# Two x tiles loaded by rows instead of columns, and their first blocks handled ahead of the rest

## The chip, the cores and the metric

The kernel runs on one NeuronCore of one Trainium2 chip. The time is the device time of one execution in microseconds; less is better. Engines are named as the profile names them: PE is TensorE, DVE is VectorE, ACT is ScalarE, POOL is GpSimd, SP is SyncE, whose queue here only issues DMAs.

## The reference: what is computed

A layernorm without scale and shift, and a two-layer MLP with a tanh GELU behind it. x is 2048 rows of 1024, the hidden width is 3584, everything is bf16 at the borders.

```python
B, S, D, F = 1, 2048, 1024, 3584
y = _layernorm(x, axis=-1)
h = _gelu(jnp.einsum("bsd,df->bsf", y, w1) + b1)
return jnp.einsum("bsf,fd->bsd", h, w2) + b2
```

## The kernel before, in words

The 2048 rows are cut into 16 tiles of 128 rows; four tiles make a block, and there are four blocks. For each block, a first stage makes the hidden values transposed: for each of 28 groups of 128 hidden columns, 8 matmuls (one per 128 of D) add up into one PSUM bank, and ACT applies bias and GELU into `hT_sb`. A second stage multiplies `hT_sb` by w2, DVE adds b2, and SP stores. All weights stay in SBUF after one load. The matmuls of the first stage need the normalised x transposed (`yT_sb`), with D on the partitions.

For blocks 1 to 3 DVE normalises and transposes in the shadow of the matmuls. Block 0 has no such shadow, so its four tiles are handled in a special way. For tiles 0 and 1, x is only centred before the matmuls; the division by the standard deviation is done later, by a multiplication of the finished PSUM rows with `rbc_sb` (the reciprocal deviations, L346). What the front of the kernel does is this.

- Loads. All four engines' programs are lists of operations with named signals. The loop at L203 loads tiles 0 and 1 in two halves each: columns 0 to 511 through SP's queue (`x0_0`, `x1_0`), columns 512 to 1023 through ACT's (`x0_1`, `x1_1`), all 128 rows, 1024 bytes a row. Behind them on SP's queue come the pieces of w1, with x2 and x3 between them (`LOADS`).
- Row sums. ACT sums columns 0 to 511 of tile 0 and then of tile 1 (L400, a copy with an accumulator, signals `sa0`, `sa1`). DVE sums columns 512 to 1023: of tile 0 by a scaled copy with an accumulator (L403, `sd0`), of tile 1 by an addition of one 256-column half to the other with an accumulator (L417, `sd1`). An accumulator is read out by an instruction of its own.
- Centring. `centre` (L410) subtracts both partial sums, already divided by 1024, from x into `c_sb`. Tile 0 is done in two pieces, blocks 0 to 1 and 2 to 7 (a block is 128 columns), and tile 1 in two, blocks 0 to 3 and 4 to 7. DVE's written order is: sum of tile 0, centring of tile 0 (both pieces), sum of tile 1, centring of tile 1 (both pieces), `bn_stats` of tile 0 (L229), tile 2 (L426 sum, L430 centring), tile 3.
- Transposes. PE transposes the 128x128 blocks of `c_sb` into PSUM (`pe_T`, L303), in the groups of `GROUPS_0`, `GROUPS_1` and `GROUPS_2` (first block, last block plus one, PSUM bank), and ACT copies each group into `yT_sb` (L309). Tile 3 is transposed by DVE and copied by DVE and ACT (L453, L462, L467).
- PE's order. 37 small matmuls on constants whose result nobody reads (`fill`, L289), the first group of tile 0, two more of these, the two other groups of tile 0, and then what `OPEN` lists: an entry `(1, None)` is all transposes of tile 1, `(2, None)` those of tile 2, and `(t0, t1, d0, d1)` is the first stage's matmuls for hidden groups 0 to 3, tiles t0 to t1-1, D-blocks d0 to d1-1 (L329). So (0, 1, 0, 2) is 8 matmuls of 128 columns, (1, 2, 0, 2) 8 more, (0, 2, 2, 6) 16 of 256, (0, 2, 6, 8) 8 of 256. Then hidden groups 4 to 7 for three tiles (384 columns), the rest of groups 0 to 7, and groups 8 to 27 with 512 columns.
- After the transposes of tile 1 ACT's list has the square of tile 1, after those of tile 2 the squares of tiles 2 and 3 (`square`, L437), with small operations of POOL behind each.

The order of DVE's later work (normalising the next blocks, the multiplications of L346, the output additions of L389) is made by a small planner from estimates of when PE and the DMAs are done; PE's clock in it starts at `T_PE_START`.

Of the kernel before, what the change touches and what calls it, by code (L numbers as in the profile page):

```python
# [5 lines left out]
ACT = mybir.ActivationFunctionType  # L6
ALU = mybir.AluOpType
# [4 lines left out]
P = 128  # L12
# [5 lines left out]
R1 = 8  # L18
N_FILL_A = 37
N_FILL_C = 2  # L20
OPEN = ((1, None), (0, 1, 0, 2), (1, 2, 0, 2), (0, 2, 2, 6), (2, None), (0, 2, 6, 8))
CEN_0 = (0, 2, 8)
CEN_1 = (0, 4, 8)
GROUPS_0 = ((0, 2, 7), (2, 5, 4), (5, 8, 5))
GROUPS_1 = ((0, 4, 6), (4, 8, 7))
GROUPS_2 = ((0, 2, 4), (2, 5, 5), (5, 8, 6))
COPY_ACT = ((0, 1), (0, 2), (0, 3), (1, 2), (1, 3), (2, 3))
LOADS = (0, 1, 2, -2, 3, -3, 4, 5, 6, 7)
NOB = 2
# [59 lines left out]
def bass_standalone__mixer_channel_mlp__prompt_kernel(  # L89
# [8 lines left out]
    xf = x.rearrange("b s d -> (b s) d")  # L98
    of = out.rearrange("b s d -> (b s) d")
    ST, D = xf.shape  # L100
# [7 lines left out]
    HC = D // 2  # L108
    NRAW = TPB
# [29 lines left out]
    with ExitStack() as es:  # L139
# [4 lines left out]
        x_sb = sb("x_sb", [P, NT, D], BF16)  # L144
        yT_sb = sb("yT_sb", [P, 2, DT, TB], BF16)
        hT_sb = sb("hT_sb", [P, FT, TB], BF16)
        o_sb = sb("o_sb", [P, NOB, D], BF16)
        b2_sb = sb("b2_sb", [P, D], BF16)
        c_sb = sb("c_sb", [P, NRAW, D], BF16)
# [10 lines left out]
        sum_sb = sb("sum_sb", [P, NRAW + 2], F32)  # L160
# [10 lines left out]
        act = _Prog("s_act")  # L171
# [6 lines left out]
        x_ev = {}  # L178

        def dma(dst, src, sig, nbytes, q=None):  # L180
            (q or sp).op(lambda e, dst=dst, src=src: e.dma_start(dst, src), sig=sig, sem="d_" + sig, inc=16)
            dma_bytes[0] += nbytes
            est[sig] = DMA_T0 + dma_bytes[0] / DMA_BYTES_PER_US
# [18 lines left out]

        for i in range(2):  # L203
            for h, q in enumerate((sp, act)):
                dma(x_sb[:, i, h * HC:(h + 1) * HC], xf[i * P:(i + 1) * P, h * HC:(h + 1) * HC],
                    f"x{i}_{h}", P * HC * 2, q)
        for o in LOADS:
            load_x_tile(-o) if o < 0 else load_w1(o)
        sp.op(None, waits=["b1z"])
# [7 lines left out]
        for b in range(2, NB):  # L217
# [4 lines left out]
                sig="ident")  # L222
# [4 lines left out]

        def op_stats(i, h):
            return (lambda e, i=i, h=h: e.bn_stats(st_sb[:, i, 6 * h:6 * (h + 1)], x_sb[:, i, h * HC:(h + 1) * HC]),  # L229
                    [x_ev.get(i, f"x{i}_{h}")], f"st{i}_{h}", 0.65)  # L230

        def op_aggr(i, to=None):
            to = rstd_sb if to is None else to
# [6 lines left out]
        y_ev = {}  # L240
# [8 lines left out]
        def ln_seq(tiles):  # L249
            seq = []  # L250
            prev = None
            for i in tiles:
                for h in range(2):
                    seq.append(op_stats(i, h))
                    if h == 0 and prev is not None:
                        seq.append(op_norm(prev))
                seq.append(op_aggr(i))
                prev = i
            seq.append(op_norm(prev))
            return seq  # L260
# [20 lines left out]
        def dve_put(o):  # L281
            dve.op(o[0], waits=o[1], sig=o[2])
# [4 lines left out]
        def fill(n, gate=None):  # L287
            for _ in range(n):
                pe.op(lambda e: e.matmul(ps[:, 0, 0:P], lhsT=one, rhs=one, start=True, stop=True),  # L289
                      waits=[gate] if gate else [])  # L290

        def pe_T(i, group, src):
            blk, t = divmod(i, TPB)
            j0, j1, bank = group
            bap = psb[:, bank, :]
            evs = yT_ev.setdefault(i, [None] * DT)
            for j in range(j0, j1):
                waits = []
                if j == j0:
                    waits = ["ident"] + ([bank_read[bank]] if bank in bank_read else [])  # L300
                if j == j0 or y_ev[i][j] != y_ev[i][j - 1]:
                    waits.append(y_ev[i][j])
                pe.op(lambda e, j=j, o=(j - j0) * P: e.transpose(  # L303
                    out=bap[:, o:o + P], in_=src[:, j * P:(j + 1) * P], identity=ident[:, :]),
                    waits=waits, sig=(f"tp{i}_{j0}" if j == j1 - 1 else None))
                evs[j] = f"te{i}_{j0}"
            psrc = bap[:, 0:(j1 - j0) * P].rearrange("p (j s) -> p j s", j=j1 - j0)
            dst = yT_sb[:, blk % 2, j0:j1, t * P:(t + 1) * P]
            act.op(lambda e, dst=dst, psrc=psrc: e.copy(out=dst, in_=psrc), waits=[f"tp{i}_{j0}"], sig=f"te{i}_{j0}")  # L309
            bank_read[bank] = f"te{i}_{j0}"  # L310
            pe_t[0] += (j1 - j0) * 0.056
# [4 lines left out]
        def new_unit():  # L316
            u = unit_n[0]
            unit_n[0] += 1
            bank = u if u < NBANK else (u - NBANK) % NRING
            w = bank_gelu.get(bank, bank_read.get(bank))  # L320
            return bank, ([w] if w else [])
# [74 lines left out]
            store_last[(ob, region)] = sev  # L396

        act.op(lambda e: e.preload_act_table(ACT.Gelu_apprx_tanh))
        for i in range(2):
            act.op(lambda e, i=i: e.activation(out=hT_sb[:, 2 * NRAW + i, :], in_=x_sb[:, i, 0:HC], func=ACT.Copy,  # L400
                                               scale=1.0 / D, accum_out=sum_sb[:, 2 * i:2 * i + 1]),
                   waits=[f"x{i}_0"], sig=f"sa{i}")
        dve_put((lambda e: e.tensor_scalar(out=o_sb[:, 0, HC:D], in0=x_sb[:, 0, HC:D], scalar1=1.0 / D, scalar2=0.0,  # L403
                                           op0=ALU.mult, op1=ALU.add, accum_out=sum_sb[:, 1:2]),
                 ["x0_1"], "sd0"))

        def centre(i, cuts):
            y_ev[i] = []
            for j0, j1 in zip(cuts[:-1], cuts[1:]):
                dve_put((lambda e, a=j0 * P, b=j1 * P: e.tensor_scalar(  # L410
                    out=c_sb[:, i, a:b], in0=x_sb[:, i, a:b], scalar1=sum_sb[:, 2 * i:2 * i + 1],
                    scalar2=sum_sb[:, 2 * i + 1:2 * i + 2],
                    op0=ALU.subtract, op1=ALU.subtract), [f"sa{i}", f"sd{i}", f"x{i}_0"], f"y{i}_{j0}"))
                y_ev[i] += [f"y{i}_{j0}"] * (j1 - j0)

        centre(0, CEN_0)
        dve_put((lambda e: e.tensor_tensor_reduce(out=o_sb[:, 1, 0:HC // 2], in0=x_sb[:, 1, HC:HC + HC // 2],  # L417
                                                  in1=x_sb[:, 1, HC + HC // 2:D], op0=ALU.add, op1=ALU.add,
                                                  scale=1.0 / D, scalar=0.0, accum_out=sum_sb[:, 3:4]),
                 ["x1_1"], "sd1"))  # L420
        centre(1, CEN_1)
        pool.op(lambda e: e.tensor_tensor(out=tot_sb[:, :], in0=sum_sb[:, 2:3], in1=sum_sb[:, 3:4], op=ALU.add),
                waits=["sa1", "sd1"], sig="tot1")

# [40 lines left out]
        def t3_act():  # L465
            for k, (src, dst) in enumerate(c3_act):
                act.op(lambda e, src=src, dst=dst: e.copy(out=dst, in_=src), waits=["t3"],  # L467
                       sig="ta3" if k == len(c3_act) - 1 else None)

        for q in range(4):  # L470
            dve_put((lambda e, q=q: e.transpose(out=b1h_sb[32 * q:32 * (q + 1), :],
                                                in_=b1r_sb[0:32, 32 * q:32 * (q + 1)]), ["b1"], f"b1t{q}"))
        dve_put((lambda e: e.tensor_copy(out=b1_sb[:, :], in_=b1h_sb[:, :]), ["b1t3"], "b1c"))
        for q in range(4):
            rsrc = rs_sb[32 * q:32 * (q + 1), :].unsqueeze(2).broadcast_to([32, NRAW, 32])
            dve_put((lambda e, q=q, rsrc=rsrc: e.transpose(
                out=rbc_sb[32 * q:32 * (q + 1), :, 32 * q:32 * (q + 1)], in_=rsrc),
                ["rstd0"] + [f"rs{i}" for i in range(1, NRAW)], f"rq{q}"))
        for q in range(4):
            f = q ^ 1  # L480
            dve_put((lambda e, q=q, f=f: e.tensor_copy(
                out=rbc_sb[32 * q:32 * (q + 1), :, 32 * f:32 * (f + 1)],
                in_=rbc_sb[32 * f:32 * (f + 1), :, 32 * f:32 * (f + 1)]), [f"rq{f}"], f"rx{q}"))
        for h in range(2):
            f = h ^ 1
            dve_put((lambda e, h=h, f=f: e.tensor_copy(
                out=rbc_sb[64 * h:64 * (h + 1), :, 64 * f:64 * (f + 1)],
                in_=rbc_sb[64 * f:64 * (f + 1), :, 64 * f:64 * (f + 1)]),
                [f"rx{2 * f}", f"rx{2 * f + 1}"], "rbc" if h == 1 else None))

        fill(N_FILL_A)
        pe_T(0, GROUPS_0[0], c_sb[:, 0, :])
        fill(N_FILL_C)
        pe_T(0, GROUPS_0[1], c_sb[:, 0, :])
        pe_T(0, GROUPS_0[2], c_sb[:, 0, :])
        pe_t[0] = T_PE_START
        wave = [new_unit() for _ in range(R0)]
        for st in OPEN:
            t = st[0]
            if st[1] is None:  # L500
                for g in (GROUPS_2 if t == 2 else GROUPS_1):
                    pe_T(t, g, c_sb[:, t, :])
                if t == 1:
                    square(1)
                else:
                    square(2)
                    square(3)
                    t3_act()
                continue
            t0, t1, d0, d1 = st  # L510
            for dt in range(d0, d1):
                for r in range(R0):
                    pe_cell(0, r, t0, t1, wave[r][0], wave[r][1] if t0 == 0 and dt == 0 else [], None, dts=[dt])
# [43 lines left out]
        while ci < len(crit) or fi < len(fills):  # L557
            take_crit = fi >= len(fills)
            if not take_crit and ci < len(crit):
                rel_f, _, blk_f = fills[fi]  # L560
                if crit[ci][0] <= max(t_dve, rel_f) + CRIT_SLACK and blk_f > crit[ci][2]:
                    take_crit = True
            if take_crit:
                rdy, o, _ = crit[ci]
                ci += 1
            else:
                rdy, o, _ = fills[fi]
# [46 lines left out]
```

## Time and profile before

| | us |
|---|---|
| median of 3 runs | 397.56 (397.53 to 397.56) |
| the profiled execution | 397.73 |
| its span, first to last instruction | 396.5 |
| PE busy | 393.6 (99%) |
| DVE, ACT, POOL busy | 160.5, 88.1, 11.0 |
| first matmul that uses data of x and w1 | 6.88 after the span's start |
| four later first and second stages each | 48.35 |

Starts are counted from the span's start. A row of the timeline gives start, length, engine, line, operation, what it writes and reads, and how many neighbours it covers; in brackets is how long the engine had been idle, and on what it waited. The chain of waits lists the work that ended last, in order of time, with start and length. The length of a matmul includes its way through the array; matmuls that follow each other overlap, so the distance from start to start is what one costs. The profile's page gives the mean granted clock of PE as 1.00.

### The profile page before, as it was taken

The numbers are of one execution on the slowest core, as the hardware profiler recorded it, in microseconds if no ns is written. First come the engines' busy times: TensorE is split into PE (matmuls) and PEld (weight loads), VectorE is DVE, ScalarE is ACT, GpSimd is POOL, SyncE is SP. The second block draws the span as 40 slices with busy tenths as digits, with TensorE's granted clock in tenths as the row PEclk, the third lists the DMA queues.
The fourth block names the chain that finished last, engine by engine and source line by source line (L and its number), as shares of the span: only waits on it lengthen the run. The fifth ranks groups of instructions, "written<-read, shape, count | busy, mean of one in ns | idle before, by whom it ended". The sixth has DMA issues, their size and how long they took to land.

```text
span 396.5 us, 4568 instructions
## 1 busy us (share of the span) xinstructions
PE 393.6 (99%) x1955; PEld 187.7 (47%) x1955; DVE 160.5 (40%) x344; ACT 88.1 (22%) x137; POOL 11.0 (3%) x29
## 2 busy tenths in 40 slices
PE   8999999999999999999999999999999999999998
PEld 8754444444444444444444444444444444444445
DVE  5968898988999505987100000001100000001011
ACT  6663430000143442000024433100003334400000
POOL 1301100001000100000000000000000000000000
DMA  7999930000000000000000000000000000000000
GB/s 265 370 386 387 387 143 13 28 26 14 28 0 0 2 0 0 29 13 28 26 13 2 0 0 2 13 13 28 15 25 15 0 2 0 0 15 26 13 28 26
DMA packets 16349, 23.62 MB, mean 60 GB/s; under 512 B 1098, under 2 KB 8778, under 8 KB 16330
## 3 DMA queue, kind: packets, MB, share of 16 engines
q1 hardware_dynamic: 16042, 23.08, 16.4%
q8 instruction: 15, 0.25, 0.3%
q10 hardware_dynamic: 288, 0.26, 0.2%
q14 instruction: 4, 0.03, 0.0%
HBM read 19.14 MB, written 4.19 MB: 59 GB/s over the span
## 4 chain that ended last, share of the span: by engine, by line
PE 98%; DVE 0%; issue 0%
PE ps L329 49%; PE ps L378 49%; PE ps L303 0%; DVE c_sb L410 0%; DVE o_sb L417 0%; DVE o_sb L389 0%; DVE sum_sb L417 0%
## 5 line engine op out<-in xcount | busy, mean ns | idle before, releaser
L329 PE MATMUL ps<-yT_sb,w_sb 128*128 128x512 bf16 (+3 forms) x968 | 194.5, 363 | 0.0
L378 PE MATMUL ps<-w_sb,hT_sb 128*128 128x512 bf16 (+2 forms) x924 | 194.1, 373 | 0.0
L329 PEld LDWEIGHTS ps<-yT_sb,w_sb 128*128 128x128 bf16 x968 | 92.6, 98 | 100.7
L378 PEld LDWEIGHTS ps<-w_sb,hT_sb 128*128 128x128 bf16 x924 | 89.3, 98 | 104.5
L349 ACT ACTIVATE hT_sb<-ps,b_sb 128x512 bf16<-128x512 f32 x112 | 76.3, 687 | 254.8 <-PE ps L329 231.6
L389 DVE TENSOR_TENSOR o_sb<-ps,b_sb 128x512 bf16<-128x512 f32 (+2 forms) x33 | 22.3, 675 | 198.8 <-PE ps L378 198.7
L276 DVE STREAM_TRANSPOSE yT_sb<-x_sb 32x256 bf16<-32x256 bf16 x192 | 83.7, 436 | 20.7 <-PE ps L329 17.7
L346 DVE TENSOR_TENSOR ps<-ps,rbc_sb 128x512 f32<-128x512 f32 x28 | 18.9, 697 | 6.4 <-PE ps L329 5.6
L229 DVE BATCH_NORM_STATS2 st_sb<-x_sb 128x6 f32<-128x512 bf16 x26 | 17.2, 670 | 0.1
L234 POOL TENSOR_TENSOR rstd_sb<-mv_sb,nhalf 128x1 f32<-128x1 f32 x12 | 6.6, 548 | 113.8 <-DVE mv_sb L237 113.8
L244 DVE TENSOR_SCALAR x_sb<-x_sb,mv_sb,rstd_sb 128x1024 bf16<-128x1024 bf16 x12 | 6.5, 543 | 2.5 <-POOL rstd_sb L234 2.0
L289 PE MATMUL ps<-const-bfloat16-1.0 128*128 128x128 bf16 x39 | 4.5, 310 | 0.8 <-PEq L599 0.8
L289 PEld LDWEIGHTS ps<-const-bfloat16-1.0 128*128 128x128 bf16 x39 | 4.1, 145 | 0.8 <-issue 0.8
L309 ACT COPY yT_sb<-ps 128x384 bf16<-128x384 bf16 (+2 forms) x8 | 3.3, 489 | 1.7 <-PE ps L303 1.7
L237 DVE BATCH_NORM_AGGREGATE mv_sb<-st_sb 128x2 f32<-128x15 f32 x13 | 2.8, 219 | 0.8
L303 PE MATMUL ps<-ident,c_sb 128*128 128x128 bf16 x24 | 2.5, 240 | 0.2 <-DVE c_sb L410 0.2
L467 ACT COPY yT_sb<-o_sb 32x256 bf16<-32x256 bf16 x6 | 2.4, 402 | 0.1
L437 ACT ACTIVATE hT_sb<-x_sb,sum_sb 128x1024 bf16<-128x1024 bf16 x2 | 2.3, 1162 | 0.0
L462 DVE COPY yT_sb<-o_sb 32x256 bf16<-32x256 bf16 x10 | 2.2, 219 | 0.2
L403 DVE TENSOR_SCALAR_CACHE_REDUCE o_sb<-x_sb 128x512 bf16<-128x512 bf16 x1 | 0.7, 687 | 3.8 <-DMA x_sb<-in_x_dram 3.8
L303 PEld LDWEIGHTS ps<-ident,c_sb 128*128 128x128 bf16 x24 | 1.8, 108 | 0.8 <-issue 0.4
L444 POOL TENSOR_TENSOR rs_sb<-ve_sb,nhalf 128x1 f32<-128x1 f32 x3 | 1.7, 559 | 0.2
(31 smaller groups left out, 17.4 us busy)
## 6 DMA issues: line engine op xcount, KB each, us to landing
w_sb<-in_w_dram SPq DMA_DIRECT2D x4, 1792.0 KB, 18.4
w_sb<-in_w_dram SPq DMA_DIRECT2D x2, 2048.0 KB, 15.8
out_dram<-o_sb SPq DMA_DIRECT2D x31, 128.0 KB, 1.7
x_sb<-in_x_dram SPq DMA_DIRECT2D x3, 1024.0 KB, 14.8
w_sb<-in_w_dram SPq DMA_DIRECT2D x8, 256.0 KB, 5.2
w_sb<-in_w_dram SPq DMA_DIRECT2D x1, 1024.0 KB, 9.0
x_sb<-in_x_dram SPq DMA_DIRECT2D x2, 256.0 KB, 5.0
x_sb<-in_x_dram ACTq DMA_DIRECT2D x2, 128.0 KB, 3.1
```

The source lines that it names most:

```text
L229: return (lambda e, i=i, h=h: e.bn_stats(st_sb[:, i, 6 * h:6 * (h + 1)], x_sb[:, i, h * HC:(h + 1) * HC]), [x_ev.get(i, f"x{i}_{h}")], f"s ...
L234: pool.op(lambda e, i=i, to=to: e.tensor_tensor(out=to[:, i:i + 1], in0=mv_sb[:, i, 1:2], in1=nhalf[:, i:i + 1], op=ALU.pow), waits=[f"mv{ ...
L244: return (lambda e, i=i: e.tensor_scalar(out=x_sb[:, i, :], in0=x_sb[:, i, :], scalar1=mv_sb[:, i, 0:1], scalar2=rstd_sb[:, i:i + 1], op0= ...
L276: res.append((lambda e, src=src, dst=dst: e.transpose(out=dst, in_=src), waits, (f"tr{i}" if lastop else None), 0.47))
L289: pe.op(lambda e: e.matmul(ps[:, 0, 0:P], lhsT=one, rhs=one, start=True, stop=True), waits=[gate] if gate else [])
L303: pe.op(lambda e, j=j, o=(j - j0) * P: e.transpose(out=bap[:, o:o + P], in_=src[:, j * P:(j + 1) * P], identity=ident[:, :]), waits=waits, ...
L309: act.op(lambda e, dst=dst, psrc=psrc: e.copy(out=dst, in_=psrc), waits=[f"tp{i}_{j0}"], sig=f"te{i}_{j0}")
L329: pe.op(lambda e, b=b, r=r, dt=dt, n0=n0, n1=n1, bank=bank: e.matmul(ps[:, bank, n0:n1], lhsT=w1_sb[:, dt, r * P:(r + 1) * P], rhs=yT_sb[: ...
L346: crit.append((est[sig], (lambda e, bank=bank: e.tensor_tensor(out=ps[:, bank, 0:n], in0=ps[:, bank, 0:n], in1=rb, op=ALU.mult), [sig, "rb ...
L349: act.op(lambda e, r=r, bank=bank: e.activation(out=hT_sb[:, r, :], in_=ps[:, bank, :], func=ACT.Gelu_apprx_tanh, bias=b1_sb[:, r:r + 1], ...
L378: pe.op(lambda e, st=st, ft=ft, c0=c0, c1=c1, bank=bank: e.matmul(ps[:, bank, 0:c1 - c0], lhsT=hT_sb[:, ft, st * P:(st + 1) * P], rhs=w2_s ...
L389: crit.append((est[sig], (lambda e, ob=ob, c0=c0, c1=c1, bank=bank: e.tensor_tensor(out=o_sb[:, ob, c0:c1], in0=ps[:, bank, 0:c1 - c0], in ...
```

## The change

The four loads of tiles 0 and 1 become row halves: rows 0 to 63 through SP's queue and 64 to 127 through ACT's, each row whole (2048 bytes). Everything that reads tile 0 or 1 now waits for both halves. Tile 0 is summed as tile 1 is: ACT takes columns 0 to 383 (`SA0`) and DVE adds the two halves of the other 640 to each other with an accumulator; tile 1 stays at 512 and 512. DVE's order becomes: sum of tile 0, centring of its blocks 0 to 1, sum of tile 1, centring of its blocks 0 to 3, then tile 0's blocks 2 to 7, then tile 1's blocks 4 to 7. PE's order is spelled out by groups in `OPEN`: after the two extra small matmuls come tile 1's first group, tile 0's second, the 8 matmuls of (0, 1, 0, 2), tile 0's third group, tile 1's second, the 8 of (1, 2, 0, 2), the 16 of (0, 2, 2, 6), tile 2, and (0, 2, 6, 8). ACT's copies follow the order of the transposes.

```diff
-OPEN = ((1, None), (0, 1, 0, 2), (1, 2, 0, 2), (0, 2, 2, 6), (2, None), (0, 2, 6, 8))
+OPEN = (("T", 1, 0), ("T", 0, 1), (0, 1, 0, 2), ("T", 0, 2), ("T", 1, 1), (1, 2, 0, 2), (0, 2, 2, 6), ("T", 2, 0), ("T", 2, 1),
+        ("T", 2, 2), (0, 2, 6, 8))
+SA0 = 384
...
-                dma(x_sb[:, i, h * HC:(h + 1) * HC], xf[i * P:(i + 1) * P, h * HC:(h + 1) * HC],
-                    f"x{i}_{h}", P * HC * 2, q)
+                h0 = h * (P // 2)
+                dma(x_sb[h0:h0 + P // 2, i, :], xf[i * P + h0:i * P + h0 + P // 2, :], f"x{i}_{h}", P * D, q)
...
-                    [x_ev.get(i, f"x{i}_{h}")], f"st{i}_{h}", 0.65)
+                    [x_ev[i]] if i in x_ev else [f"x{i}_0", f"x{i}_1"], f"st{i}_{h}", 0.65)
...
+        def sums(i, na):
+            n2 = (D - na) // 2
+            act.op(lambda e: e.activation(out=hT_sb[:, 2 * NRAW + i, 0:na], in_=x_sb[:, i, 0:na], func=ACT.Copy,
+                                          scale=1.0 / D, accum_out=sum_sb[:, 2 * i:2 * i + 1]),
+                   waits=[f"x{i}_0", f"x{i}_1"], sig=f"sa{i}")
+            return (lambda e: e.tensor_tensor_reduce(out=o_sb[:, i, 0:n2], in0=x_sb[:, i, na:na + n2],
+                                                     in1=x_sb[:, i, na + n2:D], op0=ALU.add, op1=ALU.add,
+                                                     scale=1.0 / D, scalar=0.0, accum_out=sum_sb[:, 2 * i + 1:2 * i + 2]),
+                    [f"x{i}_0", f"x{i}_1"], f"sd{i}")
...
+        sd = [sums(0, SA0), sums(1, HC)]
+        dve_put(sd[0])
+        centre(0, *CEN_0[0:2])
+        dve_put(sd[1])
+        centre(1, *CEN_1[0:2])
+        centre(0, *CEN_0[1:3])
+        centre(1, *CEN_1[1:3])
...
         fill(N_FILL_A)
-        pe_T(0, GROUPS_0[0], c_sb[:, 0, :])
+        pe_T(0, GROUPS[0][0], c_sb[:, 0, :])
         fill(N_FILL_C)
-        pe_T(0, GROUPS_0[1], c_sb[:, 0, :])
-        pe_T(0, GROUPS_0[2], c_sb[:, 0, :])
```

More of the change, by code (lines that the diff above doesn't have):

```diff
@@ L20 @@
 N_FILL_C = 2
-OPEN = ((1, None), (0, 1, 0, 2), (1, 2, 0, 2), (0, 2, 2, 6), (2, None), (0, 2, 6, 8))
+OPEN = (("T", 1, 0), ("T", 0, 1), (0, 1, 0, 2), ("T", 0, 2), ("T", 1, 1), (1, 2, 0, 2), (0, 2, 2, 6), ("T", 2, 0), ("T", 2, 1),
+        ("T", 2, 2), (0, 2, 6, 8))
+SA0 = 384
 CEN_0 = (0, 2, 8)
 CEN_1 = (0, 4, 8)
-GROUPS_0 = ((0, 2, 7), (2, 5, 4), (5, 8, 5))
-GROUPS_1 = ((0, 4, 6), (4, 8, 7))
-GROUPS_2 = ((0, 2, 4), (2, 5, 5), (5, 8, 6))
+GROUPS = (((0, 2, 7), (2, 5, 4), (5, 8, 5)),
+          ((0, 4, 6), (4, 8, 7)),
+          ((0, 2, 4), (2, 5, 5), (5, 8, 6)))
 COPY_ACT = ((0, 1), (0, 2), (0, 3), (1, 2), (1, 3), (2, 3))
@@ L398, in bass_standalone__mixer_channel_mlp__prompt_kernel @@
         act.op(lambda e: e.preload_act_table(ACT.Gelu_apprx_tanh))
[L399 to L421, printed above, removed]
+        def sums(i, na):
[7 more added lines that the diff above has]
+                    [f"x{i}_0", f"x{i}_1"], f"sd{i}")
@@ new lines, in centre @@
+        def centre(i, j0, j1):
+            dve_put((lambda e, a=j0 * P, b=j1 * P: e.tensor_scalar(
+                out=c_sb[:, i, a:b], in0=x_sb[:, i, a:b], scalar1=sum_sb[:, 2 * i:2 * i + 1],
+                scalar2=sum_sb[:, 2 * i + 1:2 * i + 2],
+                op0=ALU.subtract, op1=ALU.subtract), [f"sa{i}", f"sd{i}", f"x{i}_0"], f"y{i}_{j0}"))
+            y_ev.setdefault(i, []).extend([f"y{i}_{j0}"] * (j1 - j0))
+        sd = [sums(0, SA0), sums(1, HC)]
+        dve_put(sd[0])
+        centre(0, *CEN_0[0:2])
@@ L498, in bass_standalone__mixer_channel_mlp__prompt_kernel @@
         for st in OPEN:
[L499 to L503, printed above, removed]
+            if st[0] == "T":
+                t, g = st[1:]
+                pe_T(t, GROUPS[t][g], c_sb[:, t, :])
+                if (t, g) == (1, len(GROUPS[1]) - 1):
                     square(1)
-                else:
+                elif (t, g) == (2, len(GROUPS[2]) - 1):
                     square(2)
```

## The prediction

> **What bounds the kernel now.** I read the page from the top, then the chain of waits, then the timeline of the first 10 us engine by engine, and last the single records around each gap. The page:
>
> ```profile
> span 396.5 us, 4568 instructions
> ...
> PE 98%; DVE 0%; issue 0%
> ```
>
> TensorE is the chain for 98% of the span, so only what lies ahead of its unbroken run can be changed here. The chain of waits, in order of time (start, length, what):
>
> ```profile
> 5.78 0.42 DVE c_sb L410
> ...
> 6.25 0.40 PE ps L303 x4
> ...
> 6.67 0.38 PE ps L303 x4
> 7.05 2.77 PE ps L329 x32
> 9.82 0.45 PE ps L303 x8
> 10.26 45.89 PE ps L329 x264
> 56.15 48.35 PE ps L378 x224
> ```
>
> From 7.45 on the single records leave no gap between matmul starts: the four later stages of 48.35 are pure matmul time. The chain begins on VectorE, with the sum of x1 (L417) and the first centring of x1 (L410). So the change is worth whatever it moves the start of the 16 matmuls of 256 columns, now at 7.91, and with them tile 2's transposes at 9.65. The timeline of VectorE, ScalarE and TensorE there (start, length; a row covers neighbours of one kind):
>
> ```profile
> 3.80 0.69 DVE L403 TENSOR_SCALAR_CACHE_REDUCE o_sb<-x_sb 128x512 bf16<-128x512 bf16 x1 [3.80 <-DMA x_sb<-in_x_dram]
> ...
> 4.61 0.73 DVE L410 TENSOR_SCALAR c_sb<-x_sb,sum_sb 128x256 bf16<-128x256 bf16 x2
> 5.26 0.42 DVE L417 CUSTOM_DVE_ANT_0 o_sb<-x_sb 128x256 bf16<-128x256 bf16 x1
> ...
> 5.78 0.74 DVE L410 TENSOR_SCALAR c_sb<-x_sb,sum_sb 128x512 bf16<-128x512 bf16 x2
> ...
> 8.01 0.69 DVE L426 SCALAR_TENSOR_TENSOR o_sb<-x_sb 128x512 bf16<-128x512 bf16 x1 [0.30 <-DMA x_sb<-in_x_dram]
> ```
> ```profile
> 3.61 0.63 ACT L400 ACTIVATE hT_sb<-x_sb 128x512 bf16<-128x512 bf16 x1 [0.61 <-DMA x_sb<-in_x_dram]
> ```
> ```profile
> 5.10 0.37 PE L303 MATMUL ps<-ident,c_sb 128*128 128x128 bf16 x2 [0.17 <-DVE c_sb L410]
> 5.27 0.42 PE L289 MATMUL ps<-const-bfloat16-1.0 128*128 128x128 bf16 x2
> 5.48 1.56 PE L303 MATMUL ps<-ident,c_sb 128*128 128x128 bf16 x14
> 6.88 2.93 PE L329 MATMUL ps<-yT_sb,w_sb 128*128 128x128 bf16 x32
> ```
>
> The reader is to see three things. VectorE's first sum waits for ACT's half of x0 (3.80), ScalarE's starts earlier on SP's half (3.61). TensorE stands idle after the 37 fills (array free at 4.72, next start 5.10: 0.38), at 6.04 (0.21 for x1's first centring), at 6.49 (0.18, its second) and at 7.33 (0.12, the copy of x1's first blocks). And small matmuls start 0.107 apart until about 5.93 and 0.056 apart after it (256 columns: 0.109), though the profile's clock column says 1.00 throughout: TensorE runs at half speed for its first 5.1 us.
>
> **The change, step by step.** All starts are of the profiled execution.
>
> *Loads.* Four DMAs stay, on the same queues in the same order; each issue (0.38 to 0.47) stays. A half tile becomes 64 pieces of 2 KB instead of 128 of 1 KB. In the packet records a 1 KB packet takes 46 ns and a 2 KB one (x2, x3) 84, so each of the 16 DMA engines needs 4 x 84 instead of 8 x 46: 0.03 less per half, at best 0.06 for x0 and 0.12 for both tiles and all behind them. Nothing in the trace loads 64 partitions, so the other end is that half the partitions take data at half the rate. The page's 370 to 387 GB/s make 0.68 for x0 and 1.37 for both; doubled, x0 lands 0.68 later and x1 and all behind it 1.37 later. I take no change: both queues are in flight at once, so both halves are being filled, which is nearest the rows.
>
> [...]
>
> *Both sums now wait for both halves of x0.* ScalarE loses its early start (3.61), VectorE nothing. Two waits need one more wait instruction (0.05 in the records): both start at 3.85. VectorE's pairwise sum of 640 columns makes 320 outputs: between 0.42 (256 outputs, L417) and 0.69 (512, L403), by slope 0.48; read out by 4.34. ScalarE's 384 columns: 0.63 for 512 less 0.12 (its copies take 0.372, 0.485, 0.612 for 256, 384, 512): 0.51, and its read-out ends 0.09 later: 4.45. Centring of x0's first two blocks: 4.48 to 4.83, where it is 4.61 to 4.96. Tile 0's first transposes follow by 0.15: 4.98 instead of 5.10, then the two fills, array free at 5.38.
>
> *VectorE's new order.* x1's sum moves ahead of x0's six other blocks: 4.75 to 5.17. ScalarE's half sum of x1: x1 landed at 4.49, start 4.54, read out 5.24. Centring of x1's first four blocks: 5.28 to 5.69 (was 5.78 to 6.19); x0's rest 5.61 to 6.08 (was 4.87 to 5.34); x1's rest 6.00 to 6.41 (was 6.11 to 6.52). So x0's rest is now queued behind a wait for x1, which it was not.
>
> *TensorE's new order.* Tile 1's first four transposes at 5.75 (centring plus 0.06, as 6.19 to 6.25 now), the first two cold: done 6.06. Tile 0's next three at 6.14. Eight matmuls of tile 0 at 6.31; their copy is done by 5.8. Tile 0's last three at 6.75, tile 1's last four at 6.92. Eight matmuls of tile 1 at 7.14: their copy ends at 6.87, so the 0.12 stall goes. Then the 16 wide ones at 7.59, where they are at 7.91. ScalarE does the five copies in TensorE's order; the last, tile 1's second half, ends at 8.13, and the matmul that needs it starts at 7.59 + 8 x 0.109 = 8.46. Idle falls from 0.38 + 0.21 + 0.18 + 0.12 to 0.26 + 0.37 + 0.08.
>
> *Behind that.* The 16 wide ones end at 7.59 + 1.75 = 9.34, where they end at 9.65. Tile 2's centring ends at 9.23 (its sum starts at 8.01 on x2's landing, its centring of 0.49 at 8.74), so tile 2 can't start before 9.29: 0.05 of slack is left, and 0.36 is the most that this change can save without an earlier x2 (0.12 more at best by the packets). ScalarE's square of x1 then runs 8.05 to 9.27 and is over before tile 2's copies at 9.66. Tile 3's copies by ScalarE end at 15.85 now, 0.3 ahead of the first matmul that reads them; they follow tile 2's copies and two squares without a gap, so they come earlier by the same 0.31. bn_stats of x0 waits for nothing new. The planner's estimates of TensorE move by six transposes (0.34 us); the order that they give to VectorE comes out the same in its own arithmetic.
>
> *Sum.* −0.31 us: span 396.49 to 396.18, with the 1.24 around it 397.73 to 397.42. The profiled execution is 0.17 above the median of 397.56, so against the median 397.25. A measurement of this kernel can tell about 0.2% (0.8 us) from no change; this is 0.08%.
>
> **Rivals.** *The halves land late.* Lateness L of x1 moves the whole front, since even x0's rest now waits behind x1's sum. Break-even is L = 0.31; slower by 0.8 needs 1.1. With L = 1.37 the wide ones start at 8.96, tile 2 at 10.71: 1.05 later, 398.6. For it: no 64-row load is in the trace. Against it: ACT's halves land 3.1 us after issue and SP's 2.9, so the two streams share the engines evenly and fill both halves together. Something between, L from 0.2 to 1.0, gives 397.4 to 398.2.
>
> *TensorE stays at half speed longer* (the one on the other side). The slow phase ended at 5.93 after 5.1 us of activity with one idle stretch of 0.38. Now there are two, 0.26 and 0.37, and the second ends just before 5.93. If that restarts the count, all until about 10.85 runs cold: 30 small ones at 0.107 from 5.75 to 8.95, nine wide ones at 0.213, seven at 0.109, tile 2 at 11.63: 1.98 later, 399.5. It decides once the end of the slow phase comes 2.2 us late or more (each microsecond costs half of one, and 0.31 is gained). For it: the idle time before 5.93 grows from 0.38 to 0.63. Against it: 0.38 did no harm.
>
> [...]
>
> *Hidden anyway.* If x2 alone lands 0.36 later, tile 2's wait for VectorE takes all of the gain: 397.56. Its cause would be the same half-tile loads ahead of x2 on SP's queue, so its chance lies within the late halves'.
>
> **How the numbers follow.** Forecast as summed 0.55; halves somewhat late 0.20; fully halved 0.05; clock 0.17; unlisted 0.03. Faster by over 0.2% needs 0.8 saved where 0.36 to 0.48 is the ceiling: 0.02. Within 0.2%: 0.55 + 0.20 = 0.75. Slower: 0.05 + 0.17 + 0.01 = 0.23. The time is the likeliest case's, 397.25, its own range 397.1 (0.48 saved) to 397.5. The range goes up to 398.4: it takes in the late halves nearly whole and leaves out the clock and the full halving.
>
> **What would show it.** Right: both first sums start near 3.85; x1's first centring ends near 5.7; no idle at 7.1; the wide matmuls start near 7.6 and tile 2's transposes near 9.3, behind them and not behind VectorE. Wrong: first sums later than 4.1 (landing); starts 0.107 apart after 6 us (clock); tile 2 waiting for VectorE (x2); any new gap after 10 us.

## The result and the profile after

The changed kernel is slower: median 399.79 us over 8 runs (398.38 to 400.57) against 397.62 for the kernel before (397.47 to 398.39). The ratio of the means is 1.0045, 95% interval 1.0033 to 1.0058. Forecast were 397.25 us and, at most, 398.4.

| | before | after |
|---|---|---|
| profiled execution, us | 397.73 | 399.81 |
| span, us | 396.5 | 398.5 |
| x0 whole in SBUF / x1 whole | 3.78 / 4.49 | 3.97 / 5.58 |
| longest idle stretch of TensorE before 8 us (from start to start, less the 0.107 of one matmul) | 0.38 | 1.29 |
| matmuls reach full speed | 5.9 | 9.8 |
| tile 2's transposes start | 9.65 | 11.70 |

The chain of waits of the changed kernel (start, length, what), to set beside the one that the prediction shows:

```profile
1.38 4.21 DMA x_sb<-in_x_dram
...
5.67 0.73 ACT hT_sb L403 x2
...
6.42 0.42 DVE c_sb L412
...
6.89 0.93 PE ps L305 x7
7.82 0.85 PE ps L331 x8
8.67 0.75 PE ps L305 x7
9.42 2.44 PE ps L331 x24
11.86 0.45 PE ps L305 x8
12.31 45.89 PE ps L331 x264
58.19 48.35 PE ps L380 x224
```

From the 264 matmuls on it is the old chain, moved: they start at 12.31 instead of 10.26 and keep their 45.89, and the stages of 48.35 behind them (six, not the four that were counted ahead of the run) keep theirs. All of the loss, 2.04 us of span, lies ahead of 12.3. The chain there no longer begins on VectorE: its first long piece is a DMA of x that ends at 5.58, the half of x1 on ACT's queue. ScalarE sums x1 only then (5.67), VectorE centres it at 6.42, and TensorE starts at 6.89. The second thing to read is the lengths: at 7.82 eight matmuls of 128 columns take 0.85 and at 8.67 seven transposes 0.75, 0.107 each, where the eight transposes at 11.86 take 0.45, 0.056 each. TensorE's own timeline (start, length, what, count):

```profile
5.22 0.37 PE L305 MATMUL ps<-ident,c_sb 128*128 128x128 bf16 x2 [0.29 <-DVE c_sb L412]
5.39 0.42 PE L291 MATMUL ps<-const-bfloat16-1.0 128*128 128x128 bf16 x2
6.89 0.93 PE L305 MATMUL ps<-ident,c_sb 128*128 128x128 bf16 x7 [1.08 <-DVE c_sb L412]
7.61 1.06 PE L331 MATMUL ps<-yT_sb,w_sb 128*128 128x128 bf16 x8
```

Eight matmuls in 1.06 us, the last one's way through the array being 0.31 of it, are 0.107 apart: half speed at 7.6 us, where the kernel before had been at full speed (0.056 apart) since 5.9. So there are two facts, x1 1.09 us late and full speed 3.9 us late, and the question is whether the second follows from the first.

Theory A: the row halves land late; TensorE, with all of its work queued behind x1, is idle for 1.29 us; and that idle time keeps its clock at half speed. Rival B: the new order carries the loss. Rival C: the moment of full speed has nothing to do with the idle time.

### The profile page after: what moved, and what is told of

Same layout as the page of the kernel before. It is cut to its first block, busy times and chain, and to the rows that moved or that the text cites. A ratio compares the mean times of both kernels' runs of the same rounds, so it can differ in the third digit from the quotient of the medians.

```text
span 398.5 us, 4573 instructions
## 1 busy us (share of the span) xinstructions
PE 394.5 (99%) x1955; PEld 188.7 (47%) x1955; DVE 160.6 (40%) x344; ACT 88.4 (22%) x137; POOL 11.1 (3%) x29
## 4 chain that ended last, share of the span: by engine, by line
PE 98%; DMA 1%; ACT 0%; DVE 0%; ACTq 0%; issue 0%
PE ps L331 49%; PE ps L380 49%; DMA x_sb<-in_x_dram 1%; PE ps L305 1%; ACT hT_sb L403 0%; ACTq L183 0%; DVE c_sb L412 0%; DVE o_sb L391 0%; ACTq L78 0%
## 5 line engine op out<-in xcount | busy, mean ns | idle before, releaser
L406 DVE CUSTOM_DVE_ANT_0 o_sb<-x_sb 128x320 bf16<-128x320 bf16 (+1 forms) x2 | 0.9, 459 | 4.8 <-DMA x_sb<-in_x_dram 4.8
```

## The experiments

**Rows alone.** The kernel before, with the loads by rows and every reader waiting for both halves.

```diff
-                dma(x_sb[:, i, h * HC:(h + 1) * HC], xf[i * P:(i + 1) * P, h * HC:(h + 1) * HC],
-                    f"x{i}_{h}", P * HC * 2, q)
+                h0 = h * (P // 2)
+                dma(x_sb[h0:h0 + P // 2, i, :], xf[i * P + h0:i * P + h0 + P // 2, :], f"x{i}_{h}", P * D, q)
...
```

> The kernel before with one part of the change: x0 and x1 are loaded by 64 rows a queue, and all readers wait for both halves; sums, centring and TensorE's order stay as before. Theory A (the row halves land late, x1 about 1.1 us late, and the idle time that this gives TensorE keeps it at half speed longer): x1's first centring ends near 6.8 as in the changed kernel, tile 2's transposes start 0.65 us later than before if the speed still changes near 6, 1.9 us later if it changes near 9.8; 398.2 to 399.5 us. Rival B (the new order, with x0's rest and all of TensorE's work queued behind x1, carries the loss): 397.6 to 397.9 us, since in the old order tile 0's work covers part of the wait.

Measured: 398.53 us (398.10 to 400.09), ratio 1.0024 (1.0011 to 1.0038). x1 was whole at 5.40. The loads alone make the kernel slower, so B is not the whole cause. The size of the step was off in the profile, which is of the fastest of the eight runs (398.10): full speed was there by 5.5 (two transposes take 0.27 at 5.48, where at half speed, in the changed kernel, two take 0.37), the old order has work of tile 0 in the gap, and tile 2 started at 9.99, 0.34 later than before and not 0.65.

```profile
9.99 0.61 PE L303 MATMUL ps<-ident,c_sb 128*128 128x128 bf16 x8
```

**Order alone.** The changed kernel with the loads by columns again (the diff above, reversed).

> The changed kernel with only the loads undone: halves by columns again, everything else as changed (pairwise sum, both halves waited for, new orders). Theory A: x1 lands near 4.5 again, the idle stretch ahead of tile 1's first transposes is near 0.4 us, and the step sum of the prediction holds: about 0.3 us less than before, 397.2 to 397.4 us, if TensorE reaches full speed near 6. Rival B: the loss stays, 398.5 us or more. A third way: the two short idle stretches alone (0.26 and 0.37) delay full speed; then 398.8 us with small matmuls 0.107 us apart up to 9 us or later.

Measured: 397.58 us (397.08 to 398.67), ratio 1.0000 (0.9991 to 1.0008). The loss is gone with the row halves, and B falls as a cause of its own: the order shows no cost by columns. By rows it does make the loss larger, from 398.53 with the old order to 399.79. The expected gain of 0.3 is not there in the median, though three of the eleven runs (397.08, 397.29, 397.37) lie below the fastest of the 31 runs of the kernel before that were taken with them (397.38). The profile, of a run of 397.88, shows where the gain went, first in TensorE's timeline, then in VectorE's:

```profile
5.70 0.73 PE L305 MATMUL ps<-ident,c_sb 128*128 128x128 bf16 x7 [0.39 <-DVE c_sb L412]
...
9.79 0.62 PE L305 MATMUL ps<-ident,c_sb 128*128 128x128 bf16 x8 [0.32 <-DVE c_sb L433]
```
```profile
8.51 0.69 DVE L429 SCALAR_TENSOR_TENSOR o_sb<-x_sb 128x512 bf16<-128x512 bf16 x1 [0.95 <-DMA x_sb<-in_x_dram]
```

Tile 1's first transposes start at 5.70 and the wide matmuls at 7.55, as the prediction had it (5.75 and 7.59). But tile 2's transposes come at 9.79, where the wide matmuls would have let them start at 9.30: they wait for VectorE (0.32 us of it shows as idle), which had waited for x2. It landed at 8.48 instead of 7.99. By the landing events of the trace, which come in 16 parts for each load, 15 parts of x2 were there by 7.63 and one came 0.85 later.

**More filling.** The changed kernel, but TensorE works on constants while it waits for x1.

```diff
-N_FILL_C = 2
+N_FILL_C = 14
```

> The changed kernel with 14 instead of 2 matmuls on constants behind tile 0's first two transposes, so that TensorE is busy while it waits for x1 (12 x 0.107 = 1.28 us, against 1.29 us of idle time). Theory A: full speed comes near 6 us, as before the change, and what is left is the late landing: tile 2's transposes near 10.4 to 10.5 instead of 9.65, bound by x2; about 0.8 us more than before, 398.4 us. Rival C (the moment of full speed does not depend on the idle time, it was late for another cause): no gain over the changed kernel, 399.8 us, with 0.107 us from start to start up to 9 us or later.

Measured: 398.74 us (398.19 to 399.05), ratio 1.0023 (1.0014 to 1.0032), 1.05 below the changed kernel's median. TensorE's timeline:

```profile
5.18 1.31 PE L291 MATMUL ps<-const-bfloat16-1.0 128*128 128x128 bf16 x14
6.34 0.73 PE L305 MATMUL ps<-ident,c_sb 128*128 128x128 bf16 x7
6.90 0.61 PE L331 MATMUL ps<-yT_sb,w_sb 128*128 128x128 bf16 x8
7.35 0.55 PE L305 MATMUL ps<-ident,c_sb 128*128 128x128 bf16 x7
7.74 2.36 PE L331 MATMUL ps<-yT_sb,w_sb 128*128 128x128 bf16 x24
10.09 0.62 PE L305 MATMUL ps<-ident,c_sb 128*128 128x128 bf16 x8
```

The profile is of the fastest of the ten runs (398.19). Seven transposes take 0.55 where the changed kernel's timeline has 0.95 for the same seven, and full speed is there at 5.9. C falls: matmuls that compute nothing, put into the wait, buy back half of the loss by the medians. (The two profiles differ by more than the clock: x1 was there at 5.03 in this one and at 5.58 in the other, with the same loads.) What is left here is the late landing: tile 2 starts at 10.09, exactly 1.30 behind x2's landing at 8.79 (1.24 for VectorE's two steps and 0.06), so x2 and not x1 is what bounds it.

**Less filling, no change of data.** The kernel before with eight matmuls on constants fewer.

```diff
-N_FILL_A = 37
+N_FILL_A = 29
```

> The kernel before with 29 instead of 37 matmuls on constants at the start and nothing else changed: they end near 3.87 instead of 4.72, so TensorE is idle for 1.23 us ahead of tile 0's transposes, about what the changed kernel has ahead of tile 1's. No data comes later. Theory A: full speed slips from near 6 to 9 or 10 us; with 20 small matmuls and some wide ones at half speed tile 2 starts about 1.25 us later, 398.8 us. Rival C: nothing moves, 397.6 us.

Measured: 398.59 us (397.23 to 399.32), ratio 1.0019 (1.0009 to 1.0029). No load is touched, and about a microsecond is lost. The profile is of the slowest of the twelve runs (399.32), and it has records of the granted clock. Its stages, cut at them (stretch, length, busy time and count of TensorE, weight loads, VectorE, ScalarE and GpSimd, then granted clock, DMA share, GB/s):

```profile
0.11:3.52 3.41, 2.69 (x26) 2.73 (x27) 0.00 (x0) 1.28 (x1) 0.79 (x9) 1.00 0.33 114
3.52:6.93 3.41, 1.75 (x24) 1.20 (x22) 2.84 (x9) 2.73 (x8) 0.19 (x1) 1.00 1.05 357
6.93:10.35 3.42, 3.42 (x28) 2.97 (x26) 3.04 (x9) 2.04 (x4) 0.85 (x1) 0.50 1.08 366
10.35:13.76 3.41, 3.41 (x34) 2.75 (x32) 3.25 (x10) 2.20 (x6) 1.11 (x3) 1.00 1.10 347
```

The clock column has no record before 3.52, where it shows 1.00 by default (the matmuls there were 0.107 apart). The clock was granted in full from 3.52, taken back to half at 6.93, and given again at 10.35: steps of 3.41 us. The work in the stretch ahead of each step: 2.69 us, then full; 1.75, then half; 3.42, then full. In the changed kernel full speed came at 9.81; TensorE was busy for 2.51 us between 3.0 and 6.4, and stayed at half. So, if the work in the stretch ahead decides, an estimate from these two runs is that leaving half speed took between 2.51 and 2.69 us of 3.41. Where the steps fall differs from profile to profile: full clock came at 3.52 with less filling, near 3.87 and at 4.78 with only x1 and only x0 by rows (both further down), by 5.5 with the rows alone, near 5.9 in the kernel before and with more filling, and at 9.81 in the changed kernel's, though TensorE starts at 0.82 or 0.83 in the kernel before, in the changed one and with more and less filling. That one kernel's times lie 1 to 2 us apart would follow from it; no run shows that by itself.

The runs without a trace bear this out, for each has its mean granted clock on record. One step at half clock, once full clock has been granted, makes it 0.996 (1 - 0.5 x 3.41 / 398; on record for the profiled run above); half clock ahead of the first grant leaves no record, and the mean stays at 1.000 (the changed kernel's profiled run, at half until 9.81). Four of the changed kernel's eight runs have 0.996, those of 399.78, 400.21, 400.28 and 400.57. So have two with the rows alone (399.63 and 400.09) and one with less filling (the profiled one). Of the experiments further down, four with only x1 by rows have it (399.94 to 400.29), four with only x0 by rows (399.90 to 400.83), and the one with 1 KB pieces. None of the 76 runs of the kernel before that were taken beside the experiments has it, and none with more filling or with the order alone. Of the runs with 1.000, the changed kernel's profiled one, at half clock until 9.81, is the only one above 399.7. So a step back to half clock marks the longest times; how many of the others were granted full clock late is not on record.

**What makes the rows late.** First the pieces: whole tiles, x0 on SP's queue and x1 on ACT's, 128 rows of 2048 bytes each, with every reader waiting for its one load.

```diff
-            for h, q in enumerate((sp, act)):
-                h0 = h * (P // 2)
-                dma(x_sb[h0:h0 + P // 2, i, :], xf[i * P + h0:i * P + h0 + P // 2, :], f"x{i}_{h}", P * D, q)
+        for i, q in enumerate((sp, act)):
+            dma(x_sb[:, i, :], xf[i * P:(i + 1) * P, :], f"x{i}_0", P * D * 2, q)
...
```

> The changed kernel with x0 in one load of 128 rows of 2048 bytes on SP's queue and x1 in one on ACT's: pieces of 2 KB as in the change, but all 128 partitions in each load. If 64 partitions a load are the cause of the late landing: the issues take 0.38 to 0.47 us again instead of 0.55 to 0.88, and x0 and x1 are both there by 4.5; x0 alone a little later than before, since it shares the time with x1 (about 4.2); 397.5 to 398.2 us. If the pieces of 2 KB are the cause: issues of 0.55 us and more, x1 at 5.0 or later, 398.7 us or more.

Measured: 397.70 us (397.62 to 399.35), ratio 1.0005 (0.9996 to 1.0014); x0 was there at 4.00 and x1 at 4.22, 3.4 us after its issue at 0.78, by this row of the trace's DMA list (KB, us from issue to landing):

```profile
x_sb<-in_x_dram ACTq DMA_DIRECT2D x1, 256.0 KB, 3.4
```

Second, rows 0 to 63 and 64 to 127 again but in 1 KB pieces: each of the four loads takes 512 columns of both tiles, and the sums wait for all four.

```diff
+        xv = xf[0:2 * P, :].rearrange("(t p) d -> p t d", p=P)
+        for c in range(2):
+            for h, q in enumerate((sp, act)):
+                h0 = h * (P // 2)
+                dma(x_sb[h0:h0 + P // 2, 0:2, c * HC:(c + 1) * HC], xv[h0:h0 + P // 2, :, c * HC:(c + 1) * HC],
+                    f"x{c}_{h}", P * D, q)
...
```

> The changed kernel with four loads of 128 KB by row halves again, but each of 1 KB pieces: rows 0 to 63 (SP) and 64 to 127 (ACT), first columns 0 to 511 of both tiles, then columns 512 to 1023 of both; all sums wait for all four. The time itself says little, since x0 is only whole with the last load. If 64 partitions a load are the cause: long issues (0.55 us and more) and the last load there at 5.0 or later, as in the changed kernel. If the pieces of 2 KB are: issues near 0.42 and all there by 4.5.

Measured, one run: 401.15 us, all four there at 5.78. The issues of x, each as min/median/max in ns, first of the changed kernel, then with whole tiles, then with 64 rows of 1 KB pieces:

```profile
L183 ACTq DMA_DIRECT2D x_sb<-in_x_dram x2: 565/672/778, 0.8 to 1.4; - x2
L183 SPq DMA_DIRECT2D x_sb<-in_x_dram x2: 548/562/575, 0.8 to 1.4; - x2
```
```profile
L183 ACTq DMA_DIRECT2D x_sb<-in_x_dram x1: 411/411/411, 0.8 to 0.8; - x1
L183 SPq DMA_DIRECT2D x_sb<-in_x_dram x1: 378/378/378, 0.8 to 0.8; - x1
```
```profile
L183 SPq DMA_DIRECT2D x_sb<-in_x_dram x2: 600/652/704, 0.8 to 1.6; - x2
L183 ACTq DMA_DIRECT2D x_sb<-in_x_dram x2: 729/792/856, 0.8 to 1.6; - x2
```

Pieces of 2 KB over 128 partitions cost nothing: issues of 0.38 and 0.41, as before the change (0.38 to 0.46), and x1 there at 4.22, where by column halves it was there at 4.49. With 64 partitions the issues are long at either size (0.55 to 0.86), and x1 is late at either size (5.58 and 5.78). It is the 64 partitions, here 0 to 63 on one queue and 64 to 127 on the other; no other 64 were tried.

Third, where the lateness arises: the changed kernel with only x1 by rows, then with only x0 by rows (there the condition is `i == 0`).

```diff
-                h0 = h * (P // 2)
-                dma(x_sb[h0:h0 + P // 2, i, :], xf[i * P + h0:i * P + h0 + P // 2, :], f"x{i}_{h}", P * D, q)
+                if i == 1:
+                    h0 = h * (P // 2)
+                    dma(x_sb[h0:h0 + P // 2, i, :], xf[i * P + h0:i * P + h0 + P // 2, :], f"x{i}_{h}", P * D, q)
+                else:
+                    dma(x_sb[:, i, h * HC:(h + 1) * HC], xf[i * P:(i + 1) * P, h * HC:(h + 1) * HC],
+                        f"x{i}_{h}", P * D, q)
```

> The changed kernel with x0 by columns again and x1 by rows as in the change. It tells what makes x1 late: in the changed kernel x1's issues end 0.33 (SP) and 0.48 us (ACT) later than by columns, its landing is 0.5 to 1.1 us later. If the late issue is all: x0's issues are short again, x1's end only 0.1 to 0.2 us later than by columns, and x1 lands by 4.7; about 397.7 to 397.9 us. If the data of 64 rows also move more slowly: x1 at 5.0 or later, 398.3 us or more.

Measured: 399.94 us (397.95 to 400.29), ratio 1.0045 (1.0029 to 1.0061). x1's issues end only 0.1 later than by columns (1.77), x1 at 5.32.

> The counterpart: x0 by rows as in the change, x1 by columns. x0 is there near 3.9 to 4.1; x1's issues are short but start behind x0's long ones, 0.17 us later than by columns. If only the load's own issue and movement count: x1 by 4.8, 397.8 to 398.1 us, less than the run with x1 by rows loses if movement counts. If x0's 64 rows hold up what follows on the same 16 DMA engines: x1 at 5.0 or later, 398.5 us or more.

Measured: 399.46 us (398.23 to 400.83), ratio 1.0034 (1.0022 to 1.0047). x1, loaded by columns, at 6.22 in the profile, which is of the slowest of the eleven runs; 15 of the 16 parts of its later half were there by 5.03, and one came at 6.22. In both the second expectation held: the issue was the small part; the data of 64 rows moved slowly (218 and 255 GB/s from 2 to 5 us in these two, 295 before), and they held up the load behind them, which here has 128. The 16 DMA engines' rate from 3 to 4 us says the same (last column, GB/s; the last but one is their busy share). Before, changed, whole tiles, only x1 by rows:

```profile
3.00:4.00 1.00, 1.00 (x13) 1.00 (x11) 0.20 (x1) 0.39 (x1) 0.00 (x0) 1.00 1.09 379
```
```profile
3.00:4.00 1.00, 1.00 (x13) 1.00 (x11) 0.00 (x0) 0.47 (x1) 0.00 (x0) 1.00 0.89 186
```
```profile
3.00:4.00 1.00, 1.00 (x13) 1.00 (x11) 0.00 (x0) 0.00 (x0) 0.00 (x0) 1.00 1.05 386
```
```profile
3.00:4.00 1.00, 1.00 (x14) 1.00 (x12) 0.13 (x1) 0.27 (x2) 0.00 (x0) 1.00 0.74 195
```

In these two it is half the rate, with the engines counted as busy for 0.74 to 0.89 of the time. This microsecond shows the most: with only x0 by rows it was 245, with 64 rows of 1 KB 284. From 2 to 5 us the mean was 295 GB/s before, 297 with the order alone and 329 with whole tiles, against 238 for the changed kernel, 218 with only x1 by rows, 229 with 64 rows of 1 KB and 255 with only x0 by rows. The loss there, 238 beside 295, is smaller than in the one microsecond, 186 beside 379. Why two loads of 64 rows move their data more slowly is not shown by any run here.

**Towards a faster version.** The run with the order alone, with both of its idle stretches filled:

```diff
-N_FILL_A = 37
-N_FILL_C = 2
+N_FILL_A = 39
+N_FILL_C = 6
```

> The run with the loads by columns and the new orders, with 39 instead of 37 matmuls on constants at the start and 6 instead of 2 behind tile 0's first two transposes, which fills both idle stretches (0.3 to 0.6 and 0.5 us). If the activity window of 3.41 us that the clock rows show decides, no window from the second on has more than 0.4 us of idle time and the spread of the times shrinks from above; median 397.2 to 397.4 us, 0.3 less than the kernel before. If the idle stretches were harmless: the same as without them, 397.6 us. x2's landing stays a bound for tile 2 either way.

Measured: 397.65 us (397.18 to 398.43), ratio 1.0001 (0.9992 to 1.0009). A miss: no gain, and little less spread. In its profile TensorE waited 0.29 for w1 at 6.45, and tile 2 again waited for x2 (landed 8.50). Then the same with x2 ahead of the third piece of w1:

```diff
-LOADS = (0, 1, 2, -2, 3, -3, 4, 5, 6, 7)
+LOADS = (0, 1, -2, 2, 3, -3, 4, 5, 6, 7)
```

> As the run before, and x2 is loaded ahead of the third piece of w1 instead of behind it. If tile 2's wait for x2 (0.38 us of idle time in the profile of the run with the loads by columns) takes the gain, x2 now lands about 0.7 us earlier, tile 2 follows the wide matmuls without a gap, and the median falls below 397.3 us; if the third piece of w1 becomes the new wait (it lands near 8.2 to 8.5, needed near 8.4), 397.4 to 397.6 us.

Measured: 397.52 us (397.18 to 398.28), ratio 0.9996 (0.9987 to 1.0005). x2 was there at 6.74 and TensorE had no gap after 5.0, so the wait is gone; but in the profiled execution full speed came only near 6.7 (seven transposes from 5.80 take 0.95, the next seven, from 7.07, 0.55), and tile 2 started at 9.66. That it beats the kernel before is not shown: the interval reaches from 0.5 us faster to 0.2 us slower.

## Why the prediction was wrong, point by point

*"I take no change" (the loads).* This step failed. The lateness L of x1 that it set to zero was 1.09 in the profile and 0.54 to 1.73 in the others with row halves (the 1.73 with one part of 16 far behind the rest). The doubled end was nearer, but it is not what happened either: it had x0 0.68 late and x1 1.37, where x0 was 0.19 late and x1 1.09, and in that profile the rate fell to half for one microsecond of three. The argument against it, that both queues are in flight and so both halves are being filled, rested on rows of loads over 128 partitions, which say nothing of 64. The full halving was given 0.05.

*The rivals as alternatives.* The late halves and the longer half speed were given chances as if one excluded the other, 0.20 and 0.05 beside 0.17. The first brings on the second: a late x1 is idle time for TensorE (1.29 us), and with that time idle full speed came at 9.81, with it filled at 5.9. Neither alone gives the result; together they do. Tile 1's first transposes start at 6.89 instead of the 5.75 that was worked out: 1.14, of which L is 1.09. From there to tile 2's start the changed kernel takes 4.81 instead of 3.59 (9.34 less 5.75): 1.22, for half speed up to 9.81. Less the 0.31 of the forecast, tile 2 starts 2.05 later than before, and the span grew by 2.04. The range went up to 398.4 because the two were never taken together. The shortest of the eight runs (398.38, granted clock 1.000) would fit L with no missed step, 397.62 - 0.31 + 1.09 = 398.40; it has no trace that shows it.

*The clock.* "0.38 did no harm" was read as evidence that 0.63 would do none. In the runs 2.69 us busy in a step was enough for full clock, 2.51 was not. The prediction had a longer half speed as a rival, but the restart of a count, which it priced at 1.98, was an assumption, and the records show something else: steps of 3.41 us, the next one at 9.81 and not at 10.85. The 1.98 has the 0.31 of the forecast taken off already, so the restart alone was priced at 2.29; the longer half speed cost 1.22 here, since it ended earlier than that and the late start left less work to run at half speed. Without the late load it was seldom paid (order alone: median 397.58, no run with a clock of 0.996).

*The sums and the orders.* These terms held. The pairwise sum of 320 outputs took 0.49 (0.48 worked out), ScalarE's 384 columns 0.52 (0.51); by columns the wide matmuls start at 7.55 (7.59; full speed came earlier in that profile, by about 3.8, where eight constant matmuls take 0.63, so the agreement is in part luck). The sentence that x0's rest is now queued behind a wait for x1 was right and was the lever: by rows in the old order tile 0's transposes still fill part of the gap (398.53), in the new order nothing does (399.79).

*Tile 2's slack of 0.05.* It was taken from one execution's landing of x2. By columns, with x2 in its old place, x2 landed at 7.99 and 8.04 in two profiles with the old order and at 8.48 and 8.50 in two with the new. In the last two the wide matmuls start at 7.55 and 7.75 instead of 7.91, so all or half of the forecast's gain was there on TensorE, and it was then lost at tile 2 (9.79 and 9.80); this was the "hidden anyway" rival, cause apart. Whether the new order has a part in the later landing is not shown: the run of 397.08 with that order is 0.8 faster than the profiled one, so x2 can hardly have been as late there.

## What to carry to other kernels

Split a load between two queues by columns (or by tiles) before trying it by partitions: here, from 2 to 5 us, the profiles with loads of 64 rows show 218 to 255 GB/s where those with loads of 128 rows show 295 to 329, and a load of 128 rows behind them was whole at 6.22 (15 of its 16 parts by 5.03) instead of 4.49. A wait of a microsecond on TensorE early in a kernel can cost two, as here (x1 1.09 late, 2.04 of span lost), because in these traces the clock went with how busy TensorE was in the 3.41 us before: 2.69 us, then full, 2.51, still half; fill such a wait with matmuls that compute nothing (1.05 us less by the medians here) before judging what the wait itself costs. And where one rival brings on another, work out the case in which both happen.

## What was not expected of the hardware

- With less filling the clock was taken back after a step of 3.41 us in which TensorE was busy for half of it (1.75 us), the longest idle stretch being 1.30 us. With only x1 by rows it was taken back near 7.28, after 1.68 us of work in 3.41. With only x0 by rows it was half again from 8.19 to 11.60, after 1.19 us of work in 3.41:

```profile
4.78:8.19 3.41, 1.19 (x15) 0.74 (x14) 1.84 (x7) 1.21 (x4) 0.19 (x1) 1.00 1.00 340
8.19:11.60 3.41, 3.41 (x31) 3.10 (x29) 3.34 (x9) 2.89 (x6) 0.89 (x1) 0.50 1.07 368
```

- In these runs, issuing a load of x0 or x1 over 64 partitions occupied the queue's engine for 0.54 to 0.88 us, one over 128 partitions for 0.38 to 0.46; behind the 64-row loads of x0 the issues of x1 over 128 partitions also grew, to 0.56 and 0.83 (only x0 by rows; both issues of a queue together 1.17 and 1.43).
